# A gated mixer with a diagonal state-space layer: its first layer cut into three tiles of 128 channels and one of 64, with fill-in work in a new order

## The chip, the core and the metric

The kernel runs on one NeuronCore of a Trainium2 chip. Five engines work side by side, each with its own in-order queue of instructions: PE (TensorE, matrix products; PEld is its loading of the stationary operand), DVE (VectorE), ACT (ScalarE), POOL (GpSimd) and SP (SyncE, which here issues nearly all transfers). They wait for one another through semaphores. The metric is the time of one execution in microseconds (us) on the device. The kernel before takes 380.68 us (median of three runs, 379.26 to 380.78).

## What is computed

One sequence of 2048 tokens with 448 channels, all in float32. Two branches read the same x and are mixed by a gate that has one value for each token:

```python
x = A_u
g = _sigmoid((x * gate_w).sum(-1, keepdims=True))
a = _A_ref(x, ...)      # state-space convolution along the tokens, + x * D_skip
b = _B_ref(x, w1, w2, w3, w4)
return g * a + (1 - g) * b

def _B_ref(x, w1, w2, w3, w4):
    h = _gelu(_layernorm(x) @ w1)          # 448 x 448
    c = D // 4                             # four groups of 112 channels
    g0, g1, g2, g3 = h shifted along the tokens by +1, -1, +2, -2, group by group
    hs = concatenate([g0, g1, g2, g3]) @ w2
    x1 = x + hs
    h2 = _gelu(_layernorm(x1) @ w3) @ w4   # 448 -> 1792 -> 448
    return x1 + h2
```

Branch a is computed here through moments of the convolution's kernel and running sums along the tokens ("scans"); a general convolution stands behind a run-time test and isn't taken with this data.

## The kernel before

Tokens are worked on in four blocks of 512 (`TB`), channels on the 128 partitions. A **unit** is one block's pass through one slice of a hidden layer. Units 0 to 15 are the first layer ("a"): four blocks by four channel groups of 112, taken in the order (0, 2, 1, 3), whose shifts are +1, +2, -1 and -2. Units 16 to 71 are the second layer ("d"): four blocks by 14 slices of 128 channels.

Each float32 operand is split into a high part that PE takes at its faster rate and a low rest ("h" and "l" in names: `xh`, `xl`, `w1h`, `w1l`, ...), and three products are added: high by high, weight-low by high, weight-high by low. So a unit has two runs of matmuls:

- `first(n)` (L419): 11 matmuls of 512 columns, four slices of the 448 input channels for `xh` by weight-high and for `xh` by weight-low, and three for `xl` (the fourth slice holds 64 high and 64 low rows at once).
- `second(n)` (L482): 12 matmuls of 448 columns, four groups of 128 tokens by three products (`uh` by weight-high, `uh` by weight-low, `ul` by weight-high), added up in the four PSUM banks acc0 to acc3 over all units of a block.

Between them stand `act_mul` (L440, DVE: times the row factors `rb`, since the first layer norm's division is put behind the product), `act_head` (L448, ACT: gelu into `uf`), `act_copy` (ACT: the high part `uh`) and `act_tail` (L470, DVE: the low part `ul`). The loop at the end of `mixer_and_small_steps` issues, for each n, `second(n)` behind `first(n + 2)`, so that gelu and splitting of a unit run beside the matmuls of its neighbours.

The order of everything else is written by hand: `at(n, function, ...)` hangs a piece of fill-in work on unit n, into one of the lists `before`, `between`, `after` and `late`, which says where in the unit's code it is issued. Fill-in work is splitting of weights and inputs, means and variances (`stats_b`), the reciprocal roots `rstd` (L313: on DVE, or its 12 small steps on POOL behind two on DVE), turning of x for the second layer norm (`norm_...`), moments for branch a (`ssm_...`), and from unit `OWN` = 34 on the scans, of which `ssm_some` issues 3.9 us by its own cost numbers in each unit.

`begin` (L805) issues the opening: units 0 to 3, the first halves of units 4 and 5. There, w1 gets its column means subtracted: POOL adds up the four slices of a group (`pool_sum`), one matmul spreads the mean over the partitions (`col_means`), and DVE subtracts it (`center`). The row factors of tokens come from `rstd` into `r1`; `rstd_rows` (L333) spreads them over the partitions by transposing matmuls into PSUM, and ACT copies them to `rb`. `keep_warm` issues four matmuls whose result isn't used.

The gate's sums over channels ride along as extra columns of w1 (`GW` = 114 instead of 112): ACT copies them out (`logits`), and they go through DRAM to one transposing matmul and a sigmoid (`gates`).

Of the kernel before, what the change touches and what calls it, by code (L numbers as in the profile page):

```python
# [16 lines left out]
L = 2048  # L17
# [7 lines left out]
GW = G + 2  # L25
# [4 lines left out]
SHIFT = (1, -1, 2, -2)  # L30
EPS = 1e-5
LAG = 2
OWN = 34
# [12 lines left out]
def gated_mix_kernel(tc, x, xT, xb, x0, w1, w2, w3, w4, par, logdt, dskip, ident, parg, uflip, lags, out):  # L46
    nc = tc.nc
    with tc.tile_pool(name="keep", bufs=1) as keep:
# [3 lines left out]
        with ExitStack() as ctx:  # L52
            mixer_and_small_steps(ctx, tc, xs, gg, okm, x, xT, xb, x0, w1, w2, w3, w4, par, logdt, dskip, ident, out)
# [121 lines left out]
def mixer_and_small_steps(ctx, tc, xs, gg, okm, x, xT, xb, x0, w1, w2, w3, w4, par, logdt, dskip, ident, out):  # L175
# [16 lines left out]
    lg = dr.tile([1, L + 2], F32, name="lg")  # L192
# [16 lines left out]
    nu = big.tile([128, 4, 4], F32, name="nu")  # L209

# [30 lines left out]

    w1h, w1l = wpair([128, 4, 4, GW], "w1")
    w2h, w2l = wpair([G, 4, D], "w2")
    w1r = big.tile([128, 4, 4, GW], F32, name="w1r", tag="w4al")
    w2r = big.tile([128, 4, D], F32, name="w2r", tag="w4ah")

    def first_loads():
# [5 lines left out]
        act(w1r[:, 0], w1[:, 0])  # L253
        sp(r[:, :2 * HW], x0[:, :2 * HW])
        act(w1r[:, 2], w1[:, 2])
# [3 lines left out]
        sp(w1r[:, 1], w1[:, 1])  # L259
# [3 lines left out]
        sp(w1r[:, 3], w1[:, 3])  # L263
# [6 lines left out]
    def constants():  # L270
# [7 lines left out]
        nc.gpsimd.memset(carry, 0.0)  # L278
        nc.gpsimd.memset(rb[:, 0:HALO], 0.0)
# [53 lines left out]
    def rstd_rows(j0, j1, bank="misc"):  # L333
        p = ps.tile([128, TB], F32, name="misc", tag=bank, bufs=3 if bank == "p1" else 1)
        for j in range(j0, j1):
            nc.tensor.transpose(p[:, (j - j0) * 128:(j - j0 + 1) * 128], r1[:, j:j + 1].to_broadcast([128, 128]), idt)  # L336
        nc.scalar.activation(rb[:, HALO + j0 * 128:HALO + j1 * 128], p[:, :(j1 - j0) * 128], AF.Copy)

# [30 lines left out]
    NT_ = {}  # L369
# [9 lines left out]
    def norm_d(b, i):  # L379
        j = NT * b + i  # L380
        xn = XN[b, i] = wk.tile([128, 512], F32, name="xn", tag="xn")
        nc.scalar.activation(xn[:, :D], xs[:, j, :], AF.Identity, bias=nm[:, j:j + 1], scale=r2[:, j:j + 1])
# [11 lines left out]
    def norm_fetch(b, i):  # L394
        d = XD.pop((b, i))
        p = NT_[b, i] = wk.tile([128, 4, 128], F32, name="xr", tag="xn")
# [22 lines left out]
    def first(n, bank="p1", seq=None, stop=True):  # L419
# [3 lines left out]
        if kind == "a":  # L423
            m = GW if i < 2 else G
            wh, wl = w1h[:, i, :, :m], w1l[:, i, :, :m]
            o = HALO - SHIFT[i]
        else:
            m = 128
            wh, wl = (w[:, :, i * m:(i + 1) * m] for w in (w3h, w3l))
# [5 lines left out]
        every = [(w, x_, k, 0, TB) for w, x_, r in ((0, 0, 4), (1, 0, 4), (0, 1, 3)) for k in range(r)]  # L435
        for q, (w, x_, k, t0, t1) in enumerate(seq or every):
            nc.tensor.matmul(p[:m, t0:t1], (wl if w else wh)[:, k, :], (xl if x_ else xh)[:, k, o + t0:o + t1],  # L437
                             start=(q == 0 and fresh), stop=stop if q + 1 == len(seq or every) else False)

    def act_mul(n):  # L440

        kind, b, i = units[n]
        m = G if kind == "a" else 128
        UF[n] = wk.tile([128, TB], F32, name="uf")
        o = b * TB + HALO - SHIFT[i]
        nc.vector.tensor_mul(UF[n][:m], P1[n][:m], rb[:m, o:o + TB])  # L446

    def act_head(n, later=False):  # L448
        kind, b, i = units[n]
        m = G if kind == "a" else 128  # L450
        UL[n] = wk.tile([128, TB], F32R, name="ul", bufs=3)
        UH[n] = wk.tile([128, TB], F32R, name="uh", bufs=3)
        if kind == "a":
            if n not in UF:
                act_mul(n)
            nc.scalar.activation(UF[n][:m], UF[n][:m], AF.Gelu_apprx_tanh)  # L456
        else:
            UF[n] = wk.tile([128, TB], F32, name="uf")
            nc.scalar.activation(UF[n][:m], P1[n][:m], AF.Gelu_apprx_tanh)  # L459
        if not later:  # L460
            act_copy(n)
        p = P1.pop(n)
        if kind == "a" and n and (i == 0 or (i == 1 and b == NB - 1)):
            logits(p, b, i)
# [583 lines left out]
```

## Time and profile before

| | us |
|---|---|
| median of three runs | 380.68 |
| the profiled execution, whole | 380.4 |
| its span, first to last instruction | 378.6 |
| busy PE / DVE / ACT / POOL | 368.5 / 295.8 / 210.2 / 71.1 |
| first matmul of the work proper (unit 0) | at 7.24 |
| first matmul of `first(6)`, where the opening ends | at 38.13 |
| last addition on DVE | at 372.83 |

Times in the trace are counted from the span's start. The profiled execution's own time is 1.8 us above its span. In rows of the profile, a matmul's duration has a modelled end that overlaps the next one; how much time a matmul takes of PE is read from starts, or from runs of many in the chain of work that ended last.

### The profile page before, as it was taken

How to read it: one execution, taken by the hardware profiler on the slowest of the kernel's cores; microseconds unless marked ns; L12 is line 12 of the kernel's file. 1: busy time of each engine (PE TensorE's matmuls, PEld its weight loads, DVE VectorE, ACT ScalarE, POOL GpSimd, SP SyncE). 2: the span in 40 equal slices, each digit the busy share in tenths (PEclk: the TensorE clock that was granted, in tenths of full speed). 3: DMA queues.
4: the chain of work that ended last, by engine and by line, in shares of the span. 5: the costliest groups of instructions: out<-in, count | busy, mean ns of one | idle time of the engine just before them, and what ended most of it. 6: DMA issues, size and time to landing. Idle time of an engine off the chain costs nothing.

```text
span 378.6 us, 5180 instructions
## 1 busy us (share of the span) xinstructions
PE 368.5 (97%) x1713; PEld 314.6 (83%) x1713; DVE 295.8 (78%) x527; ACT 210.2 (56%) x349; POOL 71.1 (19%) x187
## 2 busy tenths in 40 slices
PE   7998999999999999999999999999999999999993
PEld 4786888888888888888888888888888888888883
DVE  4888979785858981998399989999787999996312
ACT  4764646546978467643465575465756654442220
POOL 3200070322000000040023536324041440000000
PEclk9999999999999999999999999999999999999998
DMA  8970606166615219000843515256685311372202
GB/s 266 397 265 1 224 1 173 30 118 209 209 56 157 46 50 214 3 0 12 243 72 78 83 29 153 63 160 124 97 183 134 78 28 19 73 189 48 77 0 102
DMA packets 85896, 42.26 MB, mean 112 GB/s; under 512 B 67030, under 2 KB 80614, under 8 KB 85226
## 3 DMA queue, kind: packets, MB, share of 16 engines
q1 hardware_dynamic: 85434, 41.20, 41.6%
q10 hardware_dynamic: 432, 0.70, 0.6%
q8 instruction: 15, 0.25, 0.3%
q14 instruction: 15, 0.12, 0.1%
HBM read 30.86 MB, written 11.02 MB: 111 GB/s over the span
## 4 chain that ended last, share of the span: by engine, by line
PE 90%; DVE 3%; ACT 2%; DMA 2%; issue 1%; POOL 0%; SPq 0%; DVEq 0%
PE p L437 46%; PE acc L499 43%; DMA w1r<-w_in 2%; PE acc L520 1%; ACT uh L468 1%; ACT uf L456 1%; PE misc L336 0%; DVE uf L446 0%; DVE z L638 0%; DVE w2l L218 0%; DVE b L286 0%; ACT w2h L217 0%; ACT xn L294 0%; DVE ul L472 0%; DVE xh L365 0%
## 5 line engine op out<-in xcount | busy, mean ns | idle before, releaser
L459 ACT ACTIVATE uf<-p 128x512 f32<-128x512 f32 x56 | 33.4, 597 | 101.9 <-PE p L437 101.8
L472 DVE TENSOR_TENSOR ul<-uf,uh 128x512 fp32r<-128x512 f32 (+1 forms) x72 | 48.9, 680 | 31.5 <-ACT uh L468 31.4
L638 DVE TENSOR_TENSOR_SCAN z<-z,carry 128x512 f32<-128x512 f32 x48 | 61.5, 1281 | 4.6 <-ACT z L633 0.7
L437 PE MATMUL p<-xh,w3h 128*128 128x512 f32 x224 | 61.3, 396 | 0.0
L437 PE MATMUL p<-xh,w3l 128*128 128x512 f32 x224 | 60.7, 392 | 0.0
L499 PE MATMUL acc<-w4h,uh 128*128 128x448 f32 x216 | 55.8, 364 | 0.3 <-DVE xs L508 0.3
L499 PE MATMUL acc<-w4h,ul 128*128 128x448 f32 x216 | 55.7, 364 | 0.0
L499 PE MATMUL acc<-w4l,uh 128*128 128x448 f32 x216 | 55.7, 363 | 0.0
L437 PEld LDWEIGHTS p<-xh,w3l 128*128 128x128 f32 x224 | 42.1, 188 | 9.9
L437 PE MATMUL p<-xl,w3h 128*128 128x512 f32 x168 | 48.0, 394 | 0.0
L437 PEld LDWEIGHTS p<-xh,w3h 128*128 128x128 f32 x224 | 42.0, 188 | 6.7
L468 ACT ACTIVATE uh<-uf 128x512 fp32r<-128x512 f32 (+1 forms) x72 | 45.6, 633 | 2.3
L499 PEld LDWEIGHTS acc<-w4h,uh 128*128 128x128 f32 x216 | 40.5, 188 | 6.6 <-issue 0.7
L499 PEld LDWEIGHTS acc<-w4l,uh 128*128 128x128 f32 x216 | 40.5, 188 | 3.1
L499 PEld LDWEIGHTS acc<-w4h,ul 128*128 128x128 f32 x216 | 40.5, 188 | 2.9
L633 ACT ACTIVATE z<-zs,nu 128x512 f32<-128x512 f32 x64 | 42.2, 710 | 0.8 <-DMA zs<-xT_in 0.4
L632 POOL COPY z<-carry 128x1 f32<-128x1 f32 x48 | 34.6, 731 | 17.4 <-DVE zs L644 17.1
L437 PEld LDWEIGHTS p<-xl,w3h 128*128 128x128 f32 x168 | 31.5, 188 | 7.2
L323 POOL TENSOR_TENSOR t<-r 128x4 f32<-128x4 f32 (+1 forms) x15 | 6.8, 453 | 133.2 <-DVE r L321 132.5
L640 POOL COPY carry<-z 128x1 f32<-128x1 f32 x48 | 14.1, 294 | 92.4 <-DVE z L638 91.5
L456 ACT ACTIVATE uf<-uf 112x512 f32<-112x512 f32 x16 | 10.1, 630 | 24.2 <-DVE uf L446 24.1
L638 DVE TENSOR_TENSOR_SCAN z<-z,carry,zero 128x512 f32<-128x512 f32 x16 | 20.0, 1247 | 0.0
(150 smaller groups left out, 496.5 us busy)
## 6 DMA issues: line engine op xcount, KB each, us to landing
zs<-xT_in SPq DMA_DIRECT2D x4, 1024.0 KB, 8.1
yd<-yt SPq DMA_DIRECT2D x56, 64.0 KB, 2.0
ysb<-yd SPq DMA_DIRECT2D x16, 224.0 KB, 3.0
out_dram<-xs SPq DMA_DIRECT2D x16, 224.0 KB, 2.8
raw<-xb_in SPq DMA_DIRECT2D x3, 1032.0 KB, 7.9
raw<-w_in SPq DMA_DIRECT2D x3, 1024.0 KB, 5.6
xd<-xt SPq DMA_DIRECT2D x16, 192.0 KB, 2.1
xr<-xd SPq DMA_DIRECT2D x16, 192.0 KB, 3.5
```

The costliest lines, as they stand in the source:

```text
L323: eng.tensor_mul(t, y, y)
L437: nc.tensor.matmul(p[:m, t0:t1], (wl if w else wh)[:, k, :], (xl if x_ else xh)[:, k, o + t0:o + t1], start=(q == 0 and fresh), stop=stop ...
L456: nc.scalar.activation(UF[n][:m], UF[n][:m], AF.Gelu_apprx_tanh)
L459: nc.scalar.activation(UF[n][:m], P1[n][:m], AF.Gelu_apprx_tanh)
L468: nc.scalar.activation(UH[n][:m], UF[n][:m], AF.Copy)
L472: nc.vector.tensor_sub(UL[n][:m], UF.pop(n)[:m], f32(UH[n][:m]))
L499: nc.tensor.matmul(ACC[j], (UL if p == 2 else UH)[n][:m, t], wl if p == 1 else wh, start=s and p == 0, stop=e and p == 2)
L520: nc.tensor.matmul(ACC[j], (UL if p == 2 else UH)[m][:, t], wl if p == 1 else wh, start=False, stop=m > n and p == 2)
L632: nc.gpsimd.tensor_copy(z4[:, m, 0:1], carry[:, k, m:m + 1])
L633: nc.scalar.activation(z4[:, m, 1:], ZS[b][:, k, :], AF.Copy, scale=nu[:, k, m:m + 1])
L638: nc.vector.tensor_tensor_scan(z, z, up, carry[:, k, m:m + 1], OP.add, OP.add)
L640: nc.gpsimd.tensor_copy(carry[:, k, m:m + 1], z[:, TB - 1:])
```

## The change

**First layer.** The group with shift +2 (code: i = 2) gives up 48 of its 112 channels (`GX` = 16 to each of the other three groups) and keeps `GD` = 64. The other three tiles are 128 channels wide now. In the tile of 64, `w1d` holds the weights' high part in 64 stationary columns and their low part in the other 64, so one run over `xh` gives both products, on partitions 0 to 63 and 64 to 127; `act_add` adds the two halves (ACT copies one, DVE adds). In its second run, `uh` holds the high part on partitions 0 to 63 and the low part on 64 to 127, and w2's rows stand twice. That unit then has 7 matmuls in `first` and 8 in `second`; the other three have 11 and 12 as before.

The 16 channels that a wide tile takes over were computed at that tile's shift and belong to shift +2, so `act_head` applies gelu to them a second time, moved by one to four tokens; the tokens at a block's edge are carried in `skew`, and those of the first block are computed by `first_tokens` and `first_skew`.

**Opening.** `pool_sum` goes; `col_means` has four matmuls on w1's slices instead of one on their sum. `act_mul_first` multiplies units 0 and 1 by row factors straight from PSUM. `keep_warm` is no longer called; `warm_up` runs 11 matmuls at the start instead of 8. The row factors of block 1 are made with POOL.

**Gate.** `logits`, their way through DRAM and the transposing matmul go. x is loaded once more (`gate_fetch`), 16 sums of products run on DVE at units 18 to 25 (`gate_sum`), and the sigmoid is exp, add, reciprocal.

**Order.** Splitting, statistics and turning are hung on other units, with ACT's and DVE's parts apart. Scans start at unit 35 with 3.75 us of their cost in each unit.

```diff
-GW = G + 2
+GX = 128 - G
+GD = G - 3 * GX
-OWN = 34
+OWN = 35
...
+        if kind == "a":
-            m = GW if i < 2 else G
-            wh, wl = w1h[:, i, :, :m], w1l[:, i, :, :m]
+            wh, wl = (w1d, None) if i == 2 else (w1h[:, TI[i]], w1l[:, TI[i]])
...
-        every = [(w, x_, k, 0, TB) for w, x_, r in ((0, 0, 4), (1, 0, 4), (0, 1, 3)) for k in range(r)]
+        every = [(w, x_, k, 0, TB) for x_, ks in ((0, (0, 1, 2)), (0, (3,)), (1, (0, 1, 2))) for w in range(2 - x_)
+                 for k in ks if not w or wl is not None]
...
+    def act_add(n, part=None):
+        p = P1[n]
+        if not part:
+            UF[n] = wk.tile([128, TB], F32, name="uf")
+            nc.scalar.activation(UF[n][:GD], p[GD:], AF.Copy)
+        if part is not False:
+            nc.vector.tensor_add(UF[n][:GD], p[:GD], UF[n][:GD])
...
+            uf, UF[n] = UF[n], big.tile([128, TB], F32, name="ug", tag="w4bl")
+            nc.scalar.activation(UF[n], uf, AF.Gelu_apprx_tanh)
+            if n:
+                nc.scalar.activation(UF[n][:GX, :o], sk[:, SKEW - o:], AF.Gelu_apprx_tanh)
+            nc.scalar.activation(UF[n][:GX, o:], uf[:GX, :TB - o], AF.Gelu_apprx_tanh)
...
     def act_tail(n):
+        if kind == "a" and i == 2:
+            nc.vector.tensor_sub(UH[n][GD:], uf[:GD], f32(UH[n])[:GD])
...
-        q = [(j, p) for p in range(3) for j in range(NT)]
+        q = [(j, p) for p in range(2 if kind == "a" and i == 2 else 3) for j in range(NT)]
...
+    def gate_sum(j):
+        t = GT.pop(j)
+        nc.vector.scalar_tensor_tensor(t, t, 1.0, GR[0], op0=OP.mult, op1=OP.mult, accum_out=gg[:, j:j + 1])
...
     def col_means(g):
-        nc.tensor.matmul(mean_bank(g), cm[:, 0:1].to_broadcast([128, 128]), PS[0][:, g], start=True, stop=True)
+        p = mean_bank(g)
+        for k in range(4):
+            c = int(k == 3)
+            nc.tensor.matmul(p, cm[:, c:c + 1].to_broadcast([128, 128]), W1R[g][:, k, :], start=k == 0, stop=k == 3)
...
-        warm_up(8)
+        warm_up(11)
...
-        for g in (2, 1, 3):
-            pool_sum(g)
...
-        keep_warm(4)
...
-        rstd(r1, NT + 1, 2 * NT + 1)
+        rstd(r1, NT + 1, 2 * NT + 1, nc.gpsimd)
...
+    for j, n in enumerate((18, 18, 18, 19, 20, 20, 20, 21, 21, 21, 21, 23, 25, 25, 25, 25)):
+        at(n, gate_sum, j)
...
+    after[9].insert(2, (rstd, (r1, j3, j4, nc.gpsimd)))
...
-                ssm_some(n, 3.9 - (2.2 if units[n][2] == NF - 1 else 0.0) - spent)
+                ssm_some(n, 3.75 - (2.2 if units[n][2] == NF - 1 else 0.0) - spent)
```

How the order of instructions changes is shown at three places. First PE, unit 1 (block 0, the group with shift +2), whose result is p_215 before and p_218 now; `pm` are the column means. Before:

```order
L437 MATMUL p_215<-xh,w1h 112x512 x4
L437 MATMUL p_215<-xl,w1h 112x512 x3
L437 MATMUL p_215<-xh,w1l 112x512 x4
L734 MATMUL pm<-wsum,cm 128x112
L437 MATMUL p_249<-xh,w1h 114x512 x4
```

Now:

```order
L463 MATMUL p_218<-xh,w1d 128x512 x4
L463 MATMUL p_218<-xl,w1d 128x512 x3
L818 MATMUL pm<-w1r,cm 128x128 x4
L463 MATMUL p_249<-xh,w1h 128x512 x4
```

Four of the unit's 11 matmuls are gone, and three matmuls for the column means have come behind it.

Second, PE at the end of the opening: the first run of units 4 and 5 (p_392 and p_423 before, p_425 and p_432 now), the transposes that spread block 1's row factors (misc from `r`), and the second run of unit 3. Before:

```order
L437 MATMUL p_392<-xh,w1h 114x512 x4
L437 MATMUL p_392<-xh,w1l 114x512 x4
L437 MATMUL p_392<-xl,w1h 114x512 x3
L437 MATMUL p_423<-xh,w1h 112x512 x4
L437 MATMUL p_423<-xh,w1l 112x512 x4
L437 MATMUL p_423<-xl,w1h 112x512 x3
L336 MATMUL misc<-idt,r_82 128x128 x4
L499 MATMUL acc_316<-w2h,uh 128x448
```

Now:

```order
L463 MATMUL p_425<-xh,w1h 128x512 x3
L463 MATMUL p_425<-xh,w1l 128x512 x3
L463 MATMUL p_432<-xh,w1d 128x512 x3
L463 MATMUL p_425<-xh,w1h 128x512
L463 MATMUL p_425<-xh,w1l 128x512
L463 MATMUL p_432<-xh,w1d 128x512
L463 MATMUL p_425<-xl,w1h 128x512 x3
L351 MATMUL misc<-idt,r_81 128x128 x4
L463 MATMUL p_432<-xl,w1d 128x512 x3
L567 MATMUL acc_328<-w2h,uh 128x448
```

The two units are woven together, and only three matmuls of unit 5 stand behind the transposes.

Third, DVE at the same place: the variances of block 1 (`st`), the two steps `v` and `r` of the reciprocal root, and what follows. Before, the nine refining steps (the last three rows, three times) follow on DVE itself:

```order
L286 BN_STATS b_375<-xs 128x6 x2
L288 BN_AGGR st<-b_375 128x2 x2
L301 TENSOR_SCALAR v<-st 128x4
L303 TENSOR_SCALAR r_82<-v 128x4
L306 TENSOR_TENSOR t<-r_82 128x4
L308 SCALAR_TENSOR_TENSOR t<-t,v 128x4
L310 SCALAR_TENSOR_TENSOR r_82<-t,r_82 128x4
```

Now:

```order
L301 BN_STATS b_379<-xs 128x6 x2
L303 BN_AGGR st<-b_379 128x2 x2
L335 TENSOR_SCALAR v<-st 128x4
L336 TENSOR_SCALAR r_81<-v 128x4
L386 TENSOR_TENSOR xh<-raw,xh 64x516
L384 TENSOR_TENSOR xl<-raw,xh 128x516 x3
L872 TENSOR_TENSOR w2l<-w2r,w2h 128x448
L539 TENSOR_TENSOR ul<-ug,uh 128x512
L497 TENSOR_TENSOR uf<-p_425,rb 128x512
```

The refining steps are now POOL's first arithmetic in the program (these four rows, three times):

```order
L338 TENSOR_TENSOR t<-r_81 128x4
L339 TENSOR_TENSOR t<-t,v 128x4
L340 TENSOR_SCALAR t<-t 128x4
L341 TENSOR_TENSOR r_81<-r_81,t 128x4
```

So DVE goes on from `r` at once with six subtractions (the low parts of block 1's input, of w2 and of unit 3), while POOL refines `r`, for which the transposes on PE wait.

More of the change, by code (lines that the diff above doesn't have):

```diff
@@ L867, in begin @@
+        rows, more = rows_of(0, NT, "acc3"), rows_of(NT, NT + 1, "acc2")
+        hi(*s2(2))
+        act_mul_first(rows)
+        lo_(*s1(3))
+        first_tokens()
+        first(3, "misc", wh_wl[3:])
+        act_head(0)
+        lo_(*s2(0))
+        first_skew()
+        act_head(1, True)
+        rows_out(rows, 0, NT)
+        rows_out(more, NT, NT + 1)
+        act_copy(1)
         act_tail(0)
-        act_head(1)
+        lo_(*s2(2))
         second(0)
         act_mul(2)
-        hi(*s2(2))
+        hi(*s2(1))
@@ L887, in begin @@
+        lo_(*s2(3))
         act_tail(3)
[L888 to L891 removed]
         load_x(2 * NT + 1, 3 * NT + 1)
@@ L1022 @@
     par = ktile(np.stack([a["A_log_A_real"], a["A_A_imag"], a["A_C_real"], a["A_C_imag"]], axis=1))
+    own = np.arange(D).reshape(4, G)
+    rows = [np.concatenate([own[2, GD + GX * TI[g]:GD + GX * (TI[g] + 1)], own[g]]) if g != 2 else own[2, :GD]
+            for g in range(4)]
     arrays = dict(
```

406 lines of the change are left out of this document (244 added, 162 removed).

## Prediction

> **What bounds the kernel.** I read the page's first part, then the busy times by stretch, then the chain that ended last.
>
> ```profile
> PE 368.5 (97%) x1713; PEld 314.6 (83%) x1713; DVE 295.8 (78%) x527; ACT 210.2 (56%) x349; POOL 71.1 (19%) x187
> ```
>
> PE is busy 97% of the span. The stretches (PE, PEld, DVE, ACT and POOL busy us in each) show where it isn't:
>
> ```profile
> 7.00:38.30 31.30, 29.35 (x145) 23.87 (x146) 26.25 (x66) 20.49 (x45) 3.71 (x8) 1.00 0.61 232
> 38.30:62.00 23.70, 23.70 (x113) 19.90 (x113) 20.53 (x45) 13.88 (x24) 7.08 (x26) 1.00 0.37 130
> 110.00:150.00 40.00, 40.00 (x187) 34.81 (x186) 27.19 (x57) 27.64 (x46) 0.00 (x0) 1.00 0.44 102
> 150.00:186.00 36.00, 36.00 (x169) 31.26 (x168) 27.00 (x69) 16.90 (x31) 4.13 (x17) 1.00 0.17 52
> 186.00:308.00 122.00, 122.00 (x566) 106.20 (x567) 110.03 (x150) 75.23 (x123) 42.99 (x84) 1.00 0.51 107
> ```
>
> From 38.30 on PE has no gap in these rows, at a granted clock of 1.00. There, a matmul more or less is time more or less. In the opening (before 38.30) PE waits, so engines beside it count too. The chain gives what a matmul takes of PE when many follow each other, since there each starts where the last one's time ends:
>
> ```profile
> 14.27 0.21 PE pm L734 x2
> 35.88 2.41 PE acc L499 x12
> 38.30 2.53 PE p L437 x11
> ```
>
> A `second` matmul takes 2.41/12 = 0.201 us, a `first` one 2.53/11 = 0.230, a column mean (two records in the trace) 0.21. The mean durations in the page's groups (364 and 396 ns) hold a tail that overlaps the next matmul; by them the saving below would come out almost twice as large.
>
> **The sum is made against the profiled execution's own 380.4 us** (span 378.6 and 1.8 around it). The median of the runs, 380.68, stands 0.28 above it, inside their spread.
>
> **Matmuls removed.** Four units (1, 5, 9, 13) lose four `first` and four `second` matmuls each. Behind the opening lie the `first` of units 9 and 13 (8 x 0.230 = 1.84) and the `second` of 5, 9 and 13 (12 x 0.201 = 2.41): **-4.25 us**, all on PE's full stretch. In the opening lie 8 x 0.230 + 4 x 0.201 = 2.64. Wider stationary operands (112 to 128 columns) are hidden:
>
> ```profile
> L499 PEld LDWEIGHTS acc<-w4h,uh 128*128 128x128 f32 x216 | 40.5, 188 | 6.6 <-issue 0.7
> ```
>
> A full one loads in 188 ns, under the 201 of the matmul that it runs beside; it would cost only where it exceeded that.
>
> **The opening.** PE's rows there, with the wait before each in brackets:
>
> ```profile
> 7.24 0.50 PE L437 MATMUL p<-xh,w1h 128*114 128x256 f32 x2 [0.89 <-ACT w1h L780]
> 10.68 0.47 PE L734 MATMUL pm<-wsum,cm 128*128 128x112 f32 x2 [0.21 <-POOL wsum L731]
> 21.34 0.88 PE L499 MATMUL acc<-w2h,uh 112*128 112x448 f32 x3 [0.33 <-ACT uh L468]
> 35.23 0.65 PE L336 MATMUL misc<-idt,r 128*128 128x128 f32 x4 [1.15 <-DVE r L310]
> 38.13 1.09 PE L437 MATMUL p<-xh,w1h 128*114 128x512 f32 x4
> ```
>
> and two prices of the engines beside it, a gelu on ACT (mean 630 ns) and a subtraction of 448 columns on DVE:
>
> ```profile
> L456 ACT ACTIVATE uf<-uf 112x512 f32<-112x512 f32 x16 | 10.1, 630 | 24.2 <-DVE uf L446 24.1
> 30.41 0.62 DVE L218 TENSOR_TENSOR w2l<-w2r,w2h 112x448 fp32r<-112x448 f32 x1 [0.77 <-ACT w2h L217]
> ```
>
> Work, from 7.24 to 38.13: -2.64 (above). Column means: eight products in this stretch instead of three, +5 x 0.21 = +1.05; the four of unit 1's tile now stand ahead of the first useful matmul, in the 0.89 us in which PE waits for ACT (4 x 0.21 = 0.84 if that cover goes). Four `first_tokens` products of 32 columns: between 0.06 each (by columns) and 0.21 (by the row of 112), I take 0.1, +0.4. `keep_warm` goes: -4 x 0.230 = -0.92. Together -2.1.
>
> Waits: the 0.21 for POOL's sums goes with them. The 0.33 for unit 0's `uh` stays: an ACT copy of the row factors (512 columns, as the gelu's 0.63) leaves its path, but a second gelu on 16 partitions enters. Two waits are new in PE's order. `second(0)` needs the banks in which the row factors lay, and ACT empties them only after unit 0's three ACT steps and unit 1's gelu: I take 0.8 (0 to 1.3). Unit 3's weight-low matmuls need a subtraction that now stands behind `act_add` and two multiplications (three steps of 512 columns, some 0.7 each by the 0.62 for 448) on DVE, while PE has transposes, tokens and four matmuls: 0.6 (0 to 1.0). The 1.15 for block 1's `r` goes in its old form; what takes its place is the next part. So waits: -0.21 - 1.15 + 0.8 + 0.6 = 0. Three more warm-up matmuls end around 5.4 to 6.0 where the first means could start at 4.8; `center` waits also for DVE, so +0.1 (0 to 0.6). **Opening without block 1's row factors: -2.0 us.**
>
> **Block 1's row factors on POOL.** This is the place that decides. PE's transposes need `r` from POOL's 12 small steps, and DVE runs six subtractions from SBUF at once behind handing `r` over. The trace shows what that does to POOL:
>
> ```profile
> 47.06 0.57 POOL L323 TENSOR_TENSOR t<-r 128x4 f32<-128x4 f32 x1 [33.70 <-DVE r L321]
> 47.71 0.20 POOL L324 TENSOR_TENSOR t<-t,v 128x4 f32<-128x4 f32 x1
> 50.51 0.20 POOL L326 TENSOR_TENSOR r<-r,t 128x4 f32<-128x4 f32 x1
> 51.02 0.69 DVE L472 TENSOR_TENSOR ul<-uf,uh 112x512 fp32r<-112x512 f32 x1
> 51.19 1.78 POOL L323 TENSOR_TENSOR t<-r 128x4 f32<-128x4 f32 x1 [0.48 <-DVE r L321]
> 51.62 1.29 DVE L363 TENSOR_TENSOR xl<-raw,xh 128x516 fp32r<-128x516 f32 x2
> 206.60 1.28 DVE L638 TENSOR_TENSOR_SCAN z<-z,carry 128x512 f32<-128x512 f32 x1
> 206.68 1.19 POOL L632 COPY z<-carry 128x1 f32<-128x1 f32 x1
> 207.80 0.67 DVE L472 TENSOR_TENSOR ul<-uf,uh 128x512 fp32r<-128x512 f32 x1
> ```
>
> Undisturbed, a step takes 0.20 and the next starts 0.28 later (ten steps from 47.71 to 50.51). The same step takes 1.78 where three DVE subtractions follow one another: it ends just after the last of them, at 52.97. The copy at 206.68 ends at 207.87, just after the scan beside it and inside the next DVE step. So a POOL step waits at least for the DVE step that runs; sometimes for the series.
>
> DVE's series is four subtractions of 0.69, one of 0.62 and one of 0.69, starts some 0.06 closer: 3.8 us. PE can't reach the transposes earlier than 3.0 after `r`, since the `xl` matmuls ahead need the first four of the series (2.7 and a matmul). POOL's chain then takes:
> - undisturbed 12 x 0.28 + 0.1 = 3.5, a wait of 0.5;
> - one step for each of the six DVE steps, then six at 0.28: 3.8 + 1.7 = 5.5, a wait of **2.5**;
> - kept out for the whole series: 3.8 + 3.4 = 7.2, a wait of 4.2.
>
> I take 2.5: a step that slips in at each change of DVE's instruction is what the row at 206.68 shows, and the row at 51.19 shows the longer one. PE's queue behind the transposes holds three matmuls and `second(3)`, ready by then, so the wait isn't made up. The same chain for block 3's rows (issued in unit 9, needed at unit 11) runs beside more subtractions than before: 0 to 1.4, I take 0.5. **+3.0 us.**
>
> [...]
>
> **Hidden parts.** The gate: 16 sums of products and their accumulator reads on DVE.
>
> ```profile
> L668 DVE SCALAR_TENSOR_TENSOR xs<-ysb,gg,xs 128x448 f32<-128x448 f32 x16 | 10.1, 672 | 0.0
> L594 DVE DVE_READ_ACCUMULATOR mw<-mw 128x1 f32 x12 | 1.0, 82 | 0.0
> 93.64 0.16 PE misc L554
> ```
>
> 16 x (0.672 + 0.082) = 12.1 us in units 18 to 25, the stretch 110 to 150, where DVE is busy 27.19 of 40: 39.25 then, just covered, with 9 us of room in the 36 behind it. I take 0; a lack of cover is the slower rival below. The transposing matmul (0.16) goes: **-0.2**. Its loads (16 x 224 KB) run where the DMA engines are 44% busy. ACT gains one step of at most 0.63 in each unit (the second gelu, or the copy for `act_add`) and two short ones at a block's edge; over the five units from 38.30 to 62.00 that is 3.2 us and a little, where ACT is busy 13.88 of 23.70.
>
> Scans: one unit later (4.95 us) and 0.15 of 3.9 less in each of some 24 units, another 3.6 us of scan work, about a unit; the last additions follow one unit sooner. Before, they end 14 us ahead of the end:
>
> ```profile
> 345.24 0.71 DVE L653 STREAM_TRANSPOSE yt<-zs 128x512 f32<-128x512 f32 x1
> 357.55 1.27 DVE L668 SCALAR_TENSOR_TENSOR xs<-ysb,gg,xs 128x448 f32<-128x448 f32 x2
> 372.83 0.68 DVE L524 SCALAR_TENSOR_TENSOR xs<-acc,gs,xs 128x448 f32<-128x448 f32 x1 [0.53 <-PE acc L520]
> ```
>
> They move to about 363; cost 0. It would cost from the point where they pass 372.
>
> **Sum:** -4.25 - 2.0 + 3.0 - 0.2 = -3.45; 380.4 - 3.4 = **377.0 us**.
>
> **The rivals.**
> - POOL undisturbed: +0.5 instead of +3.0, so -5.95: **374.4**. For it: the steps at 47.71 to 50.51. Against: the first steps at 47.06 and 51.19.
> - POOL kept out for the whole series and late again for block 3: 4.2 + 1.4, -0.85: **379.5**, no change by what a measurement of this kernel can tell (0.5%, 1.9 us). For it: the row at 51.19.
> - Slower: DVE becomes the bound in units 18 to 25. The gate sums stand ahead of `ul` steps in DVE's queue, and PE's second runs wait for `ul`. It decides from 5.3 us of excess (3.4 + 1.9), when DVE needs 45.3 us in those 40, 6 more than counted, by waits for the loaded x: **382.5** and more. Against: DVE runs 110.03 of 122.00 in the scans with PE full.
> - The matmuls cost what they did (the change doesn't save): would give 377.0 + 4.25 + 2.64 = 383.9. Against: PE's time goes by columns in all three chain rows; I give it almost nothing.
>
> **How the numbers follow.** Chances: the forecast 0.50 (its own range 375.8 to 378.4), POOL undisturbed 0.22, kept out 0.17, DVE bound 0.05, and 0.06 for an opening that gains 2 us more than reckoned (its waits at their lower ends). The range reaches from just under the undisturbed case to the kept-out one: 373.6 to 379.6. Faster by over 0.5% (under 378.5): 0.46 + 0.22 + 0.06 and the rest's edge, 0.75; within 0.5%: 0.18; slower 0.07.
>
> **What would show it.** In the profile after: PE matmuls 16 fewer at each of the two lines, runs of 7 and 8 in the chain; the transposes for block 1 with a wait of about 2.5 us on POOL (0.5 or 4.2 by the rivals), POOL steps there of 0.5 to 0.7 us; `first(6)` starting near 38.6; no PE gap in units 18 to 25. Wrong would be: waits on PE for `ul` around the gate sums, or the last additions to x behind PE's last matmul.

## The result, and the profile after

The changed kernel takes 375.71 us (median of 4 runs, 374.95 to 375.73) where the kernel before takes 380.62 (4 runs beside it, 379.26 to 380.78): a ratio of 0.9874, 95% interval 0.9848 to 0.9900. In a second set of runs it was 374.98 against 380.18, ratio 0.9859 (0.9839 to 0.9879). The forecast was 377.0, with 373.6 to 379.6 around it.

The profiled execution took 375.73 with a span of 374.0, against 380.4 and 378.6: 4.7 us less. The first part of its page gives busy time, share of the span and instructions of each engine:

```profile
PE 364.1 (97%) x1705; PEld 313.0 (84%) x1705; DVE 307.8 (82%) x561; ACT 214.7 (57%) x377; POOL 72.8 (19%) x197
```

Behind the opening the chain of the changed kernel shows the runs of 8 and 7 matmuls that the change was to leave (start, duration, what):

```profile
38.69 2.51 PE p L463 x11
...
46.17 1.61 PE acc L567 x8
...
53.25 1.64 PE p L463 x7
```

The busy times by stretch (PE, PEld, DVE, ACT and POOL, then the granted clock) have no gap on PE there:

```profile
38.00:88.00 50.00, 50.00 (x236) 43.32 (x235) 43.33 (x85) 37.16 (x74) 11.97 (x38) 1.00 0.37 93
110.00:150.00 40.00, 40.00 (x187) 34.69 (x185) 36.43 (x89) 20.98 (x35) 0.00 (x0) 1.00 0.51 134
186.00:308.00 122.00, 122.00 (x567) 105.97 (x566) 109.70 (x148) 72.64 (x120) 41.01 (x80) 1.00 0.48 106
```

The opening is where it is less plain. These are PE's rows there: the warm-ups (`pw`), two rows of column means (`pm`; 4.81 is where the first of them starts before), the first useful matmul, and every one with a wait (in brackets):

```profile
1.32 4.87 PE L854 MATMUL pw<-warm 128*128 128x512 bf16 x11 [1.32 <-POOL cm L286]
5.98 1.06 PE L862 MATMUL pm<-w1r,cm 128*128 128x128 f32 x4
...
7.88 1.00 PE L818 MATMUL pm<-w1r,cm 128*128 128x64 f32 x8
8.69 0.48 PE L463 MATMUL p<-xh,w1h 128*128 128x256 f32 x2
...
20.88 1.19 PE L463 MATMUL p<-xh,w1l 128*128 128x512 f32 x4 [0.41 <-DVE w1l L872]
...
23.14 0.47 PE L567 MATMUL acc<-w2h,uh 128*128 128x448 f32 x1 [0.67 <-ACT rb L355]
...
34.92 0.65 PE L351 MATMUL misc<-idt,r 128*128 128x128 f32 x4 [1.93 <-POOL r L341]
```

The first useful matmul starts 1.45 us later than before (8.69 against 7.24), and yet `first(6)`, the chain's run at 38.69, comes only 0.39 later than its counterpart at 38.30. The same stretch, first useful matmul to `first(6)`, of the kernel before and of the changed one:

```profile
7.24:38.30 31.06, 29.35 (x145) 23.87 (x146) 26.00 (x66) 20.25 (x44) 3.47 (x8) 1.00 0.61 231
```

```profile
8.69:38.69 30.00, 26.99 (x149) 22.74 (x149) 25.68 (x62) 21.12 (x49) 5.98 (x17) 1.00 0.79 297
```

PE's work there falls by 2.36 (29.35 to 26.99) and its waits grow from 1.71 to 3.01. From `first(6)` to the start of the last block's 24 matmuls (367.94 before, 363.54 after) the time is 4.79 less, and 0.2 less from there to the end of the span. So 1.45 - 1.06 - 4.79 - 0.2 = -4.6, the difference of the spans. The experiments ask what the 1.45 is, whether POOL's steps wait as reckoned, and what the matmuls and the cover on DVE are worth.

### The profile page after: what moved, and what is told of

Same layout as the page of the kernel before. It is cut to its first block, busy times and chain, and to the rows that moved or that the text cites. A ratio compares the mean times of both kernels' runs of the same rounds, so it can differ in the third digit from the quotient of the medians.

```text
span 374.0 us, 5244 instructions
## 1 busy us (share of the span) xinstructions
PE 364.1 (97%) x1705; PEld 313.0 (84%) x1705; DVE 307.8 (82%) x561; ACT 214.7 (57%) x377; POOL 72.8 (19%) x197
## 4 chain that ended last, share of the span: by engine, by line
PE 94%; DVE 2%; POOL 1%; ACT 1%; issue 1%; ACTq 0%; POOLq 0%
PE p L463 47%; PE acc L567 43%; PE pw L854 1%; PE acc L590 1%; PE pm L818 1%; DVE b L301 1%; PE misc L351 0%; POOL t L339 0%; POOL t L338 0%; DVE uf L497 0%; PE pm L862 0%; POOL r L341 0%; POOL t L340 0%; ACT rb L355 0%; DVE uf L483 0%
## 5 line engine op out<-in xcount | busy, mean ns | idle before, releaser
L463 PE MATMUL p<-xh,w3l 128*128 128x512 f32 x224 | 70.0, 394 | 0.0
L463 PE MATMUL p<-xh,w3h 128*128 128x512 f32 x224 | 69.9, 393 | 0.0
L539 DVE TENSOR_TENSOR ul<-uf,uh 128x512 fp32r<-128x512 f32 x56 | 38.2, 681 | 20.0 <-ACT uh L529 19.8
L529 ACT ACTIVATE uh<-uf 128x512 fp32r<-128x512 f32 x56 | 35.4, 632 | 1.8
L703 POOL COPY z<-carry 128x1 f32<-128x1 f32 x48 | 33.0, 699 | 16.0 <-DVE zs L715 15.9
L567 PE MATMUL acc<-w2h,uh 128*128 128x448 f32 x64 | 19.4, 366 | 0.7 <-ACT rb L355 0.7
```

The lines of the kernel that those rows point to most:

```text
L463: nc.tensor.matmul(p[:, t0:t1], (wl if w else wh)[:, k, :], (xl if x_ else xh)[:, k, o + t0:o + t1], start=(q == 0 and fresh), stop=stop i ...
L529: nc.scalar.activation(UH[n], UF[n], AF.Copy)
L539: nc.vector.tensor_sub(UL[n], uf, f32(UH[n]))
L567: nc.tensor.matmul(ACC[j], (UL if p == 2 else UH)[n][:, t], wl if p == 1 else wh, start=s and p == 0, stop=e and p == 2)
L703: nc.gpsimd.tensor_copy(z4[:, m, 0:1], carry[:, k, m:m + 1])
```

## The experiments

Since the start turned out to differ between executions, the runs are compared by two lengths that don't hold it, taken from each profile: from the first useful matmul (T0) to block 1's transposes, and from T0 to the start of the last 24 matmuls. All times in us:

| kernel | median (range) | T0 | T0 to transposes | T0 to the last 24 |
|---|---|---|---|---|
| before | 380.62 (379.26 to 380.78) | 7.24 | 27.99 | 360.70 |
| before, 11 warm-ups | 380.48 (379.83 to 381.45) | 7.17 | 28.01 | 360.20 |
| changed | 375.71 (374.95 to 375.73) | 8.69 | 26.23 | 354.85 |
| changed, again | 374.98 (374.30 to 376.06) | 7.45 | 26.26 | 356.45 |
| 8 warm-ups | 374.80 (374.60 to 374.96) | 7.73 | 26.35 | 354.98 |
| 8 warm-ups, again | 375.81 (374.65 to 377.63) | 7.75 | 26.22 | 354.85 |
| matmuls put back | 380.31 (379.39 to 381.86) | 8.00 | 26.23 | 359.16 |
| row factors on DVE | 374.62 (373.90 to 374.86) | 8.31 | 25.46 | 354.04 |
| subtractions halved | 374.52 (374.09 to 375.13) | 7.45 | 25.42 | 354.05 |
| subtractions merged | 375.72 (375.48 to 377.13) | 8.62 | 26.66 | 355.28 |
| gate sums twice | 378.25 (376.99 to 381.05) | 7.64 | 26.22 | 357.23 |
| 3.9 of scans | 377.97 (377.33 to 379.43) | 7.30 | 26.27 | 358.93 |
| longer wait | 378.68 (378.23 to 379.92) | 7.91 | 28.47 | 358.62 |
| rows on DVE, reordered | 373.97 (373.55 to 374.37) | 7.39 | 23.99 | 353.42 |

Kernels whose opening is the same agree in the fourth column within 0.15 us (26.22 to 26.35, seven of them), with starts from 7.30 to 8.69. That makes it a finer measure than the total. In the last row the transposes stand three matmuls earlier in PE's order, so its fourth column can't be set against the others. The fifth column is finer than the total too, but a half clock behind a wait is still in it, as the second profile of the changed kernel shows further down.

### The matmuls put back

```diff
+        for c in {6: (D,) * 4, 9: (TB, D) * 4, 13: (TB, D) * 4}.get(n, ()):
+            nc.tensor.matmul(p[:, :c], wh[:, 0, :], xh[:, 0, o:o + c], start=True, stop=True)
```

> The changed kernel with the matmuls that it lost behind the opening put back as matmuls whose result is overwritten: 8 of 512 columns and 12 of 448, in units 6, 9 and 13. The output stays the same. Theory (TensorE's time goes by columns, and there is no gap to hide them): 8 x 0.230 + 12 x 0.201 = +4.25, 380.0 us. Rival 1 (a matmul costs its recorded duration, 394 and 366 ns): +7.5, 383.2. Rival 2 (TensorE waits for others there anyway): under +2, below 377.7.

380.31; from T0 to the last 24 matmuls 359.16 against 354.85, +4.31 for a forecast of 4.25. A matmul on PE's full stretch costs what it takes in the chain, 0.230 and 0.201, and not its recorded 0.39 and 0.37 (by these it would have been 7.5). This is most of what the change gains.

### Block 1's row factors: what POOL waits for

Three edits at the same place. The first takes the row factors off POOL:

```diff
-        rstd(r1, NT + 1, 2 * NT + 1, nc.gpsimd)
+        rstd(r1, NT + 1, 2 * NT + 1)
```

> The changed kernel with block 1's twelve POOL steps replaced by DVE's nine at the same place of the order (eleven DVE steps of 0.2 us altogether, two of them there already). Theory (each POOL step waits for the DVE step beside it, so POOL's chain takes 5.5 us where DVE's takes 1.8 more than now): r is ready near 31.3, the subtractions move back by 1.8 to 1.9, the last xl matmul ahead of the transposes goes at 33.9, the transposes start near 34.2 instead of 34.92: 375.0 (-0.7), and no wait on POOL is left. Rival: the wait passes whole to the subtractions and on to unit 3's second run: 375.7 or up to 376.5.

The second cuts each of the four subtractions beside POOL's steps in two; the third merges three of them into one:

```diff
-            nc.vector.tensor_sub(lo[:, k, :], raw[b][:, k, :], f32(h[:, k, :]))
...
+        for t in (slice(0, XW // 2), slice(XW // 2, XW)) if b == 1 else (slice(0, XW),):
...
+                nc.vector.tensor_sub(lo[:, k, t], raw[b][:, k, t], f32(h[:, k, t]))
```

```diff
-        split_lo(1, 0)
+        h, lo = XH["a", 1], XL["a", 1]
+        nc.vector.tensor_sub(lo, raw[1][:, :3, :], f32(h[:, :3, :]))
         second(2)
-        split_lo(1, 1)
-        split_lo(1, 2)
```

> The changed kernel with the four subtractions of block 1's split, each cut into two of half the columns: eight DVE steps of some 0.4 us instead of four of 0.69. Theory (a POOL step gets in at each change of DVE's instruction): the POOL steps beside the halves last 0.35 to 0.45 us instead of 0.52 to 0.70, eight of them beside the eight halves, two beside the last two DVE steps, two undisturbed; r is ready near 34.4, the time 375.2 to 375.7. Rival 1 (POOL is kept out for the whole series): one POOL step of 3 us and more, r near 36.5. Rival 2 (POOL and DVE share the access word by word): the POOL steps stay at 0.5 to 0.7.

> The changed kernel with three of block 1's four subtractions (128x516 each) merged into one of 128x1548, some 1.9 us. Theory (a POOL step waits for the DVE step that runs): the second POOL step lasts about 1.9 us, only four of the twelve are disturbed, eight follow at 0.28, r is ready near 35.4 instead of 34.86 and the wait of the transposes grows by 0.5: 376.2. Rival (word by word): POOL steps of 0.5 to 0.7 beside it, r near 34.9, 375.7.

In the changed kernel itself POOL's and DVE's rows stand like this:

```profile
29.41 0.70 POOL L338 TENSOR_TENSOR t<-r 128x4 f32<-128x4 f32 x1 [6.41 <-DVE r L336]
...
31.53 0.52 POOL L341 TENSOR_TENSOR r<-r,t 128x4 f32<-128x4 f32 x1
...
32.66 0.53 POOL L339 TENSOR_TENSOR t<-t,v 128x4 f32<-128x4 f32 x1
33.27 0.19 POOL L340 TENSOR_SCALAR t<-t 128x4 f32<-128x4 f32 x1
...
34.66 0.20 POOL L341 TENSOR_TENSOR r<-r,t 128x4 f32<-128x4 f32 x1
```

```profile
29.36 0.69 DVE L386 TENSOR_TENSOR xh<-raw,xh 64x516 fp32r<-64x516 f32 x1
30.08 1.91 DVE L384 TENSOR_TENSOR xl<-raw,xh 128x516 fp32r<-128x516 f32 x3
31.91 0.61 DVE L872 TENSOR_TENSOR w2l<-w2r,w2h 128x448 fp32r<-128x448 f32 x1
32.45 0.68 DVE L539 TENSOR_TENSOR ul<-ug,uh 128x512 fp32r<-128x512 f32 x1
```

Six POOL steps of 0.46 to 0.70 beside six DVE instructions, then six of 0.2 when DVE has none left. POOL's rows with the subtractions merged, and the merged DVE instruction:

```profile
30.13 1.72 POOL L339 TENSOR_TENSOR t<-t,v 128x4 f32<-128x4 f32 x1
31.94 0.45 POOL L340 TENSOR_SCALAR t<-t 128x4 f32<-128x4 f32 x1
```

```profile
30.02 1.77 DVE L982 TENSOR_TENSOR xl<-raw,xh 128x1548 fp32r<-128x1548 f32 x1
```

and with them halved (POOL, then the eight DVE instructions in two rows):

```profile
28.71 0.26 POOL L339 TENSOR_TENSOR t<-t,v 128x4 f32<-128x4 f32 x1
29.06 0.37 POOL L340 TENSOR_SCALAR t<-t 128x4 f32<-128x4 f32 x1
29.52 0.25 POOL L341 TENSOR_TENSOR r<-r,t 128x4 f32<-128x4 f32 x1
```

```profile
28.15 0.77 DVE L387 TENSOR_TENSOR xh<-raw,xh 64x258 fp32r<-64x258 f32 x2
28.95 2.12 DVE L385 TENSOR_TENSOR xl<-raw,xh 128x258 fp32r<-128x258 f32 x6
```

A POOL step lasts 1.72 beside a DVE instruction of 1.77, 0.70 beside one of 0.69 and 0.26 beside one of 0.35 (2.12/6). Here it gets in where DVE's instruction changes (the step of 1.72 ends at 31.85, the instruction of 1.77 at 31.79), which is what the forecast's "one step for each of the six DVE steps" says, and neither "undisturbed" nor "kept out for the whole series". Sharing word by word, the other rival, is out too, since it would have left the step beside the merged instruction at 0.5 to 0.7. Two steps of the kernel before don't follow this: those at 51.19 (1.78) and 82.31 (1.71) lasted through three and two DVE instructions. None of the small steps of `rstd` in the changed kernel's profile did, and no run shows what sets those two apart. The transposes move with POOL's steps: 0.43 later when merged (0.5 expected), 0.81 sooner when halved (0.46 expected; the halves cost DVE only 0.3 more, and the steps beside them took 0.24 to 0.43 where 0.35 to 0.45 was expected). DVE pays nothing visible: its six instructions run from 29.36 to 33.13, 3.77 us, and take the same 3.77 (30.75 to 34.52) in the kernel with the row factors on DVE, where POOL has no step beside them.

With the row factors on DVE the transposes come 0.77 sooner (0.7 expected), and what waits is now the subtractions:

```profile
31.50 0.50 PE L463 MATMUL p<-xh,w1h 128*128 128x512 f32 x1 [0.31 <-DVE xh L386]
...
32.30 1.64 PE L463 MATMUL p<-xl,w1h 128*128 128x512 f32 x3
33.77 0.60 PE L351 MATMUL misc<-idt,r 128*128 128x128 f32 x4
```

The three `xl` matmuls, 0.86 us in the changed kernel, take 1.64, since each waits for its subtraction; `r` had been there since 30.72. The time came out at 374.62 (375.0 expected).

### The start

```diff
-        warm_up(11)
+        warm_up(8)
```

> The changed kernel with 8 warm-up matmuls at the start instead of 11. In its trace the first useful matmul starts at 8.69 (7.24 in the kernel before), because the 11 warm-ups hold TensorE until 6.19 (8 of them to 4.81). Theory: everything in the opening hangs on that start (the first unit's product, then its row factors, then ACT and DVE), so the 1.4 us come back whole: first(6) near 37.3 instead of 38.69, 374.3 us. Rival 1: the three extra warm-ups are needed and the matmuls behind run slower without them (0.43 us each instead of 0.22): half or all of the gain is lost, 375.0 to 375.7. Rival 2: the opening hangs on something later, such as the arrival of the x rows or w2: 375.7, no change.

> The kernel before with 11 warm-up matmuls instead of 8 and nothing else: what this one part of the change costs by itself. Theory (the start carries through): 380.6 + 1.4 = 382.0. Rival (hidden, as the prediction had it with +0.1): 380.6 to 380.8. Second rival: the longer warm-up makes the matmuls behind it faster, under 380.2.

> The changed kernel itself once more, beside the next two on one chip. The profiles so far show that the moment at which TensorE goes from one warm-up matmul in 0.427 us to one in 0.215 differs between executions of the same first instructions (near 4 us in one, after 6 in another), and that the opening behind the first useful matmul lasts the same (26.2 to 26.3 us to block 1's transposes) in all of them. Theory: the profiled execution of the changed kernel (375.73, first useful matmul at 8.69) was a late one; over more executions the times spread over 374.2 to 375.8 and the median falls to some 375.0 to 375.3. Rival: 11 warm-ups always end at 6.2, the median stays 375.7 and the spread is under 0.5.

> The changed kernel with 8 warm-up matmuls instead of 11 once more, beside the changed kernel on the same chip. Theory (8 hold TensorE to 4.7 at most, and what follows is then slow only where the switch comes late): gains 0 in executions that switch early and up to 1 us in those that switch late, the median 0.3 to 0.6 below that of the changed kernel. Rival 1 (the whole 1.4): 1.0 and more below. Rival 2 (the warm-ups cost nothing either way, as in the kernel before): within 0.2.

With 8 instead of 11 the changed kernel took 374.80 in one set of runs and 375.81 in another, where the changed kernel beside it took 374.98; the kernel before with 11 took 380.48 against 380.71 (ratio 0.9995, 0.9981 to 1.0008). So by the totals neither the whole 1.4 nor a settled part of it belongs to the number of warm-ups. (Two of the six executions behind 375.81, at 377.50 and 377.63, had a mean granted clock of 0.991 against 0.998 in the profiled one.) What differs most is the execution. The warm-up rows of the kernel with the halved subtractions, whose first instructions are those of the changed kernel:

```profile
1.32 3.85 PE L855 MATMUL pw<-warm 128*128 128x512 bf16 x11 [1.32 <-POOL cm L286]
...
7.45 0.48 PE L464 MATMUL p<-xh,w1h 128*128 128x256 f32 x2
```

Eleven warm-ups took 3.85 us here and 4.87 in the changed kernel's profile. A warm-up follows the one before after 0.427 us until some moment, and after 0.215 from then on. The trace records a rise of TensorE's clock at that moment, at 4.00 in this execution and at 7.19 in the other, where the column means behind the warm-ups were slow too. (The clock column of the profile's views shows 1.00 even ahead of the rise; the spacing of the warm-ups shows that it was half.) In the changed kernel with 11 warm-ups T0 then lies anywhere between 7.30 and 8.69, and the opening moves with it one for one. The number of warm-ups counts where the rise is late: with rises at 5.72 and 5.75 T0 was 7.73 with 8 and 8.00 with 11, with rises at 4.43 and 4.34 it was 7.39 and 7.30. Each of these is one profile. Over the profiles the moment lay between 4.00 and 7.19; no run shows what sets it.

### The same wait, with and without a half clock behind it

The second profile of the changed kernel started early (7.45) and ended no sooner (span 374.3). PE's rows, and the busy times of two stretches of 3.41 us that follow each other (the column behind the five engines is the clock):

```profile
33.71 0.65 PE L351 MATMUL misc<-idt,r 128*128 128x128 f32 x4 [1.95 <-POOL r L341]
...
36.32 0.57 PE L567 MATMUL acc<-w2l,uh 128*128 128x448 f32 x1
```

```profile
31.54:34.96 3.42, 1.47 (x9) 1.12 (x9) 0.38 (x1) 0.57 (x1) 1.61 (x7) 1.00 0.74 222
34.96:38.37 3.41, 3.41 (x11) 3.02 (x10) 3.31 (x6) 3.18 (x8) 0.00 (x0) 0.50 0.22 85
```

After the wait of 1.95 us the matmuls start 0.37 apart instead of 0.20, from 34.9 to 38.2: some 1.6 us lost beside the wait (356.45 against 354.85 in the table). The wait of 1.93 in the first profile had no such trail. The last run makes the wait longer:

```diff
-        for _ in range(3):
+        for _ in range(5 if j0 == NT + 1 else 3):
             eng.tensor_mul(t, y, y)
```

> The changed kernel with two more Newton iterations of block 1's row factors on POOL (eight more steps at 0.28 us, undisturbed by then): TensorE's wait ahead of the transposes grows from 1.95 to some 4.2 us. In one profiled execution of the changed kernel that wait of 1.95 was followed by 3.3 us at a granted clock of 0.50 (1.5 us lost), in another of the same kernel the wait of 1.93 was not. Theory (a long enough stretch without matmuls halves the clock for some 3.3 us afterwards; 1.95 us is at the edge, 4.2 is past it): a clock of 0.50 behind the wait in the profile, and 2.2 + 1.5 us more than the undisturbed time of some 374.6: 378 to 378.7 in nearly all executions. Rival (the half clock has nothing to do with the wait): 2.2 more, 376.8 to 377.3, at a clock of 1.00.

```profile
36.38 1.12 PE L351 MATMUL misc<-idt,r 128*128 128x128 f32 x4 [4.15 <-POOL r L341]
```

```profile
32.87:36.28 3.41, 0.00 (x0) 0.00 (x0) 0.00 (x0) 0.00 (x0) 2.43 (x13) 1.00 0.90 303
36.28:39.70 3.42, 3.33 (x11) 2.91 (x12) 0.95 (x2) 1.49 (x3) 0.04 (x1) 0.50 0.00 1
```

The wait grew by 2.22 and the kernel, from T0 on, by 3.77; all ten executions lie at 378.23 or above. So the half clock follows from the wait. A wait of about 1.95 seldom brings it: it stands, at 1.92 to 1.97, in seven profiles (the two of the changed kernel, the two with 8 warm-ups, matmuls put back, gate sums twice, 3.9 of scans), and one of the seven had the trail. The longer wait of 2.37, with the subtractions merged, had none either.

What divides them can be read from the traces. In these profiles the clock falls a whole number of 3.41 us behind its rise at the start: 9 times in the second profile of the changed kernel (4.24 to 34.96), 9 with the longer wait (5.57 to 36.28), 89 with 3.9 of scans (4.34 to 308.12), and it comes back after 3.41. PE's busy time in steps of 3.41 us, counted from the rise, tells the waits apart. Behind every step with 1.47 us or less the clock was half, in all fourteen profiles, the idle steps at the end of the kernel included; behind none with 1.49 or more was it. These are two steps with the same wait in the opening and no half clock behind them, from the kernel with 3.9 of scans (a wait of 1.97) and from the first profile of the changed kernel:

```profile
31.64:35.06 3.42, 1.49 (x9) 1.34 (x10) 0.30 (x2) 0.71 (x2) 1.38 (x7) 1.00 0.80 259
```

```profile
31.09:34.50 3.41, 1.90 (x9) 1.19 (x7) 2.04 (x4) 0.00 (x0) 2.76 (x9) 1.00 0.24 46
```

The wait of 2.37 fell across two steps, with 1.97 and 2.49 of busy time in them. So by these profiles what decides is how much of a wait falls into one step of 3.41 us, and that changes with the moment of the rise. This fits all the profiles but was found in them afterwards; no run shifts the steps on purpose, and since the ends of matmuls are modelled, 1.47 and 1.49 aren't sharp. The changed kernel's own times, 374.3 to 376.1, hold both the start and this trail.

### DVE's cover in units 18 to 25

```diff
         t = GT.pop(j)
+        nc.vector.scalar_tensor_tensor(t, t, 1.0, t, op0=OP.mult, op1=OP.max, accum_out=gg[:, j:j + 1])
```

> The changed kernel with a second DVE instruction of the same size ahead of each of the 16 gate sums (its result is overwritten, the output stays the same). In the trace the sums start 0.545 us apart, so that is 8.7 us more of DVE in units 18 to 25, where DVE is busy 36.43 of the 40 us from 110 to 150. Theory (the cover there is almost used up; DVE becomes the bound as the slower rival had it): 8.7 less the 3.6 left is 5 us, 379 to 382, with waits of PE for ul. Rival (units wait for one another loosely enough that the quieter stretch behind, 150 to 170, takes it up): 376 to 377.

378.25, less than the theory and more than the rival. The profile is of the fastest of the eight executions (376.99), in which 2.4 more passed from T0 on than in the first profile of the changed kernel. PE's rows with a wait:

```profile
136.37 1.08 PE L567 MATMUL acc<-w4h,uh 128*128 128x448 f32 x4 [0.32 <-ACT w4h L870]
138.97 1.09 PE L567 MATMUL acc<-w4l,uh 128*128 128x448 f32 x4 [1.52 <-DVE w4l L873]
```

Of the 8.7 us all but some 2 went into gaps and later units in this execution. DVE does become the bound, but the first to suffer is the splitting of the w4 weights behind the sums, at one place, and no unit's `ul`. The three slowest executions (379.29 to 381.05) had a mean granted clock of 0.987 to 0.993 against 0.998 in the profiled one; half clock behind waits would fit that, but no profile shows where it lay.

### The scans

```diff
-                ssm_some(n, 3.75 - (2.2 if units[n][2] == NF - 1 else 0.0) - spent)
+                ssm_some(n, 3.9 - (2.2 if units[n][2] == NF - 1 else 0.0) - spent)
```

> The changed kernel with 3.9 us of scan work for each unit again instead of 3.75. In the kernel before, PE waited some 0.5 us around 310 for DVE's additions to x at the end of a block, behind a scan; in the changed one it doesn't. Theory (the fewer scans took that wait away): a wait of 0.2 to 0.5 us at a block's end comes back, 376.0 to 376.2. Rival (it is a matter of where the scans happen to fall, or of the order elsewhere): 375.7 with no gap.

377.97, and 4.1 more from T0 on, where the theory had 0.3 to 0.5. DVE's rows and PE's at a block's end, and the step of 3.41 us with the wait and the one behind it:

```profile
303.85 2.70 DVE L709 TENSOR_TENSOR_SCAN z<-z,carry 128x512 f32<-128x512 f32 x2
306.46 2.43 DVE L578 SCALAR_TENSOR_TENSOR xs<-acc,gs,xs 128x448 f32<-128x448 f32 x4
```

```profile
307.26 0.45 PE L567 MATMUL acc<-w4h,uh 128*128 128x448 f32 x1 [2.24 <-DVE xs L578]
```

```profile
304.71:308.12 3.41, 1.17 (x6) 0.84 (x5) 3.28 (x5) 3.03 (x5) 1.57 (x4) 1.00 0.12 19
308.12:311.54 3.42, 3.42 (x10) 3.02 (x10) 3.35 (x6) 0.04 (x1) 0.77 (x2) 0.50 0.00 0
```

Two scans stand ahead of the four additions that empty the accumulators, PE waits 2.24, and the half clock behind it takes most of the rest. In the kernel before, with its 3.9 and an earlier begin of the scans, PE waited 0.28 at this place in one profile:

```profile
310.54 0.44 PE L499 MATMUL acc<-w4h,uh 128*128 128x448 f32 x1 [0.28 <-DVE xs L508]
```

and not at all in the other (with 11 warm-ups). So 3.75 isn't worth 4 us against the kernel before; in the new order it keeps this wait away. Whether the later begin of the scans or another part of the order makes 3.9 cost so much there, no run separates.

### Rows on DVE, with the order of the matmuls to match

```diff
-        warm_up(11)
+        warm_up(8)
...
-        rstd(r1, NT + 1, 2 * NT + 1, nc.gpsimd)
+        rstd(r1, NT + 1, 2 * NT + 1)
...
-        first(4, seq=[(0, 1, k, 0, TB) for k in range(3)])
         rstd_rows(NT + 1, 2 * NT + 1)
-        first(5, seq=[(0, 1, k, 0, TB) for k in range(3)])
+        for k in range(3):
+            for n in (4, 5):
+                first(n, seq=[(0, 1, k, 0, TB)], stop=k == 2)
```

> The changed kernel with 8 warm-ups, block 1's rows computed on DVE (nine small steps instead of POOL's twelve), the transposes right behind the twelve matmuls that need only w1 and xh, and then the xl matmuls of units 4 and 5 in turn. From the profile with the rows on DVE: r is ready 0.1 before TensorE's wait of 0.31, and TensorE waits 0.8 more in unit 4's xl matmuls; with transposes and unit 5's matmuls in those gaps the second run of unit 3 starts at 33.9 to 34.2 instead of 34.9 there. Theory (DVE bounds this stretch, POOL's steps did no good): 0.8 + 0.7 less than the changed kernel from the first useful matmul on, and the start as in the kernel beside it: 373.2 to 373.8 us. Rival (the gain is given back at unit 3's ul or at the row factors of unit 4): as with the rows on DVE alone, 374.3 to 374.7.

```profile
30.58 0.49 PE L463 MATMUL p<-xh,w1h 128*128 128x512 f32 x1 [0.30 <-DVE xh L386]
...
31.38 0.60 PE L351 MATMUL misc<-idt,r 128*128 128x128 f32 x4
...
32.98 0.39 PE L463 MATMUL p<-xl,w1d 128*128 128x512 f32 x1
```

373.97 (373.55 to 374.37), ratio to the kernel before 0.9836 (0.9817 to 0.9854), beside 374.98 of the changed kernel on the same chip. From T0 on its profile is 1.43 shorter than the changed kernel's first one; 1.5 was expected. No wait over 0.3 is left between 28 and 39, nor any half clock in its profile.

## Why the prediction was right, point by point

- **Matmuls removed, -4.25.** Right: 4.22 by the chain (0.80 for each of three runs of 8, 0.91 for each of two of 7), 4.31 put back.
- **The opening's total, +0.5.** It came out at +0.39, but by two errors that cancel, and that is luck. The start was given +0.1 (0 to 0.6) and was +1.45 in the profiled execution; in executions where the clock rises early it is 0.1 to 0.2 (7.30 to 7.45 against 7.24). The end of the warm-ups was within the range given (the next matmul at 5.98); what failed is the cover behind it. The 0.89 us in which PE waited before were to hide unit 1's column means and the longer warm-ups both. In the profiled execution those means filled them (7.88 to 8.69), PE ran without a wait from the warm-ups to the first useful matmul, and so the late end of the warm-ups and the slow means behind them (5.98 to 7.23, where they took 4.81 to 5.54 before) came through. The other error is in the waits, below.
- **The opening's work, -2.1.** 2.36 less from the first useful matmul on, with unit 1's column means ahead of it.
- **The opening's waits.** Each of the three came, each smaller: 0.41 for unit 3's `w1l` (0.6), 0.67 for the row factors' bank (0.8), 1.93 for POOL's `r` (2.5). The 0.33 for unit 0's `uh`, which was to stay, went. Together 1.30 more than before, where 2.54 was reckoned. POOL's chain was sized right, 29.41 to 34.86 = 5.45 for 5.5; PE came to the transposes some 0.6 later than the earliest moment the sum had used, held by the matmuls ahead of them in its own queue.
- **Block 3's rows, +0.5 (0 to 1.4).** No wait: PE's transposes there start at 71.29, POOL's last step ends at 70.86. The step failed by taking the middle of a range whose lower end was true.
- **Gate.** The transposing matmul's 0.16 went. The sums cost DVE 8.7 us (they start 0.545 apart where DVE runs them in a row) and not 12.1, so it was busy 36.43 of the 40 and not 39.25. PE had no gap there. The rival of DVE as the bound is real, but of 8.7 us more of DVE work some 6 were still taken up in the profiled execution. (Its 382.5 is a slip of the sum: 377.0 and 5.3 us of excess are 382.3.)
- **Scans, 0.** Held for the last additions (the last pair starts at 358.08, 357.55 before, with the end 4.4 sooner). The wait of 0.28 at the block's end, with 0.25 more in the run behind it (2.67 for 2.41), was in the profile before and not counted; after it is gone. (It is also absent from the profile of the kernel before with 11 warm-ups, so it doesn't come in every execution.) That, block 3's 0.5 and 0.2 at the tail are most of the difference between 377.0 and 375.7.
- **The rivals.** The measured 375.71 is just under the forecast's own range (375.8 to 378.4) and as near to POOL undisturbed (374.4) as to 377.0, so the total doesn't choose between the two. POOL undisturbed even lies inside the changed kernel's spread of times, and is refuted all the same: the POOL rows decide, and the halved and merged subtractions, not the total.

## What to carry to other kernels

Small steps on POOL beside a series of two-input DVE subtractions cost one DVE instruction each here (0.46 to 0.70 us for a step that took 0.20 with none beside it), in two cases of the kernel before two and three (1.71 and 1.78); if another engine waits for their end, put them on DVE (0.77 sooner here), or see that the DVE instructions are short (0.81 sooner with four of them halved). Compare changes of a few tenths from a point in the trace behind the start, not by the total, when the start itself varies by over a microsecond. And count a TensorE wait of about 2 us and more not as its length alone but as possibly some 1.6 us more: seldom at 2 (one profile of seven here), in all ten executions, by their times, at 4.15.

## What the runs showed of the hardware

- A wait of 1.95, 2.24 or 4.15 us on TensorE was followed by 3.41 us at half clock, in which 448 columns take 0.37 instead of 0.20; six waits of 1.92 to 1.97 were not, nor one of 2.37 with the subtractions merged. Counted in steps of 3.41 us from the clock's rise, half clock came behind each step with 1.47 us or less of matmuls (43% of it) and behind none with 1.49 or more, in fourteen profiles. An estimate from these figures: a single wait under some 1.9 us (3.41 less 1.49) wouldn't bring it, one over some 3.9 (twice the 1.94 of 3.41 less 1.47) would, and between them it would depend on where the wait falls. A step need not be idle for it: 1.47 us of matmuls in one were too few.
- The moment at which TensorE's clock rises lay between 4.00 and 7.19 us after the start in executions with the same first instructions, and moved the first useful matmul by up to 1.4 us. In the profiles of the kernel before it came early both times (4.46 and 4.50); whether that is chance stays open.
- A step of 128x4 on POOL beside a series of two-input DVE subtractions ended with the DVE instruction that ran, 1.72 beside one of 1.77 (two steps of the kernel before, 1.78 and 1.71, ended with a later one), and the series took the same 3.77 us with and without POOL's steps.
